# An S4 layer gated by a feed-forward block, forward and backward on one core: some transposing loads turned on TensorE, two dx chunks added in place, another order of the work

## The chip, the cores and the metric

The kernel runs on one core of a Trainium2 chip. The metric is the device time of one execution in microseconds. The time before is the median of three runs.

## The reference

The input `x` is 2048 rows of 512. It is layer-normed to `xn`; `xn` goes through an S4 convolution (a kernel of length 2048 for each of 512 channels, built from 128 complex states) and through a feed-forward block 512 to 1792 to 512. The output is `x + s * silu(ffn)`. The kernel returns this output and its gradients by `x`, by the six parameter arrays of the states (512 by 128 each), by the step and skip vectors and by both weights, for a given `grad_out`.

```python
def _A_ref(u, A_re, A_im, B_re, B_im, C_re, C_im, log_dt, Dskip):
    dt = jnp.exp(log_dt)[:, None]
    logdA, dB = dt * (A_re + 1j * A_im), dt * (B_re + 1j * B_im)
    P = jnp.exp(logdA[:, :, None] * arange(L))
    K = jnp.einsum("dn,dnl,dn->dl", C_re + 1j * C_im, P, dB).real
    y = irfft(rfft(pad(u)) * rfft(pad(K)))[:L]
    return y + u * Dskip

def _fwd(x, ...):
    xn = layernorm(x)
    s = _A_ref(xn, ...)
    g = silu(silu(xn @ w1) @ w2)
    return x + s * g

out, vjp = jax.vjp(_fwd, x, ...)
return (out, *vjp(grad_out))
```

## The kernel before

**Layout.** Rows are held as 128 partitions by 16 row tiles `t`, the 512 columns as four blocks of 128 (`b`, or `dk` and the like), the 1792 hidden columns as 14 tiles `ft`. The convolution is done by matrices of a discrete Fourier transform (`dft_fwd`, `cplx_mul`, `dft_inv`). Intermediates that don't fit on the chip go to DRAM and come back: `Hd` (hidden before silu, stored with hidden columns on the partitions), `DHd` (its gradient, in the same layout), `Pd` (the feed-forward part of the gradient by `xn`), `Yd` and `Ed` (powers of the state factors), `dKd` (gradient of the convolution kernel).

**Streams and order.** The work is written as generators, each named by one letter. A generator yields after each step, a step being a group of instructions, often for one engine. Seven strings, `PLAN[0]` to `PLAN[6]`, list the letters in the order in which the steps are issued; `play` walks through a string and advances the named generator by one step. Each engine carries out its instructions in the order in which they are issued, and SP, which issues most of the DMAs, does too. `SLOTS` fixes which of its buffers each tile takes, and `WAYS` says for each eviction made by `k.ev` whether ACT (`A`, line 112 in the profile) or DVE (`D`, line 113) makes it.

**Stages.** `PLAN[0]` is set-up and the start of the feed-forward block, `PLAN[1]` and `PLAN[2]` the forward convolution and the rest of the feed-forward block, `PLAN[3]` the backward convolution (`B`), the output (`O`) and the backward feed-forward block (`A`, `x`). The change touches mostly what follows.

- `gen_dx` (`x`, line 1166): sixteen row tiles of `dhT` times `W1`. Each result is evicted to `pd_s` and stored in `Pd`. `gen_conv_bwd` (`B`) writes the other part of the gradient by `xn`, called du, into `k.ds` on the chip.
- `gen_ssm_loads` (`Y`, line 970): sixteen groups `(b, h, q0)`. For each a tile `YT` is loaded from `Yd` by two transposing DMAs, and for each second group `Eb` from `Ed`. `gen_ssm_fold` (`N`) makes `Gf` from `dKd`.
- `gen_ssm_v` (`V`, line 996): `YT` times `Gb` into the PSUM tile `ps_v` (pool `pc`, two buffers), evicted to `Vb`.
- `gen_ssm_products` (`T`, lines 1012 and 1017): complex products of `Vb` with `Eb` on DVE, four multiplications into `Tp` and `Tq` and two sums, six instructions a group.
- `gen_ssm_sums` (`S`, line 1034): `Tp` summed over its `NE` = 21 exponents by matmuls with the identity, two exponents at a time (eleven matmuls), into `psS`, copied to `Sa`. `gen_ssm_grads` (`Z`) adds the two halves of `Sa` (line 1059) and makes the six state gradients and that of the step.
- `gen_dw2_loads` (`h`), `gen_dw2_turns` (`t`) and `gen_dw2` (`w`, line 1206): for each `ft`, `h_in` is loaded from `Hd`, brought to rows on the partitions, put through silu into `a_tok`, and multiplied with `k.do`. The tiles `ft` 0 to 8 are loaded plain (line 1182) and turned by sixteen TensorE transposes (line 134), with silu from PSUM in two halves (line 1197); 9 to 13 are loaded by a transposing DMA (line 1180), with silu in one piece (line 1194).
- `gen_dw1_loads` (`g`, line 1221) and `gen_dw1` (`v`, line 1235): `dh_tok` comes from `DHd` by transposing DMAs, two for each of seven pairs, and is multiplied with `xn`.
- `gen_ln_loads` (`i`), `gen_ln_sums` (`k`, lines 1270 to 1277) and `gen_ln_rows` (`m`): the backward layer norm, in eight chunks of two row tiles. Chunks of `Pd` come back as `pd_l`; line 1270 adds `k.ds` on DVE and sums the row in the same instruction.

`PLAN[4]` mixes the end of `A` and `x` with the start of `N Y V T S`, `PLAN[5]` the rest of these with `Z h t w g v`, `PLAN[6]` the end of `t w g v` with `i k m`. The tiles of `i k m` take the memory of those of `N Y V T S Z`.

Of the kernel before, what the change touches and what calls it, by code (L numbers as in the profile page):

```python
# [18 lines left out]
P = 128  # L19
# [8 lines left out]
122p13273555417652067776357p577511777p747701636770773677J0J767p5787777367F66766767077F78676777633FF736746687F46F8F7486FF  # L28
F8F6666FF6F688FF56F64FJ8/XFXQFJFFFXXXPJXPXFXPFFFPXPXFPFPFQJFFFQQF9QQQFFFXFQFJQQXXQPFQXRPFFRXPXRRXFXPPFRFXPJFRRXFRPXFRQQQ
RPXQFQRQFXFRQQFFRFUFFXFQXFFFFRQRXRPRFRQXRRJPRRUPFPXRRURFRPRURQRXRFJRQCRPQFXXXXFFRQXXXQFQFQQXPQRPPFCRCCCFFFRCRCQRPCRQFRFC  # L30
RFFRFFPQRQCUQFRCFFFFCQQRFFCCQQCFCQFCXRCQQCFQCRPXFFCRXCFXCFXFPXCRPFXFCXRFCXRFJCFRRCXRPCXCFRFFQQCFRFCQQFCFRQPFFCRQPRRFCPQC
QFXFRQQRPQRCXRRRCXXJPRXRRXCUPXPRXXRCRFCPCCRQQPFFCFCFFCCPQCQFFQCRRQQCQRRXFQFCXFRFFCFQFCFCFCCCCPQJRRXCXRCCFCFFXPRRCXFPCRXC
CFCXQQCQFFQJRXPQFRCCQXCCCRQFRFQFCPRQCQRRRRRQRRRXRFPCFXRPFRFCXRCXPFURRRCXCFFRRXCCFFQFQJQQCXFXCFFCCRQCFFRCCRQQCQRFQCFRCRRR
RRCCCCXRQCCCCRCJRCRCRURRFCRRFCRCCRFFCCCCRC/CGCFCCGCCGFGFFFCCFCGCCGFGCCFGGCFCFFCGCGFCCGFCFWGCGGGGCGCFCHFCFGCGHFCCFCFCCGCH
FCGCWWCFCCCGGCWCWCCCWWHCCWCDHWHHGCCWDGMCCCWHCWWDWWDWDWLDGDWWDWWWWLWDMDDDMDDDLDDMLLWM/DEWDadDodDEDdDsBDADAAAoBDaDADdaAAAo
AsDBAoBABDWDWABADBBAasBoAAAoBBBAAAAlOBBADOaABoAADlOBBBsBxBoBDoBBDBBDEABABxDOABABxOABBBBAsxBODBoxDBxdOOBloDBoDOBxBaxDBBBD
# [17 lines left out]
101010101010101010101010101010101010101010101010101010101010101010110101010101011010101010101010101010101010101010101;tb
l.tv=01011101010110100010110100011010;tbl.ts=01010101110111010101001000101010;tbl.W=01010101010010100101;dft.t4=01001010
1010;gate.g=30124567;gate.S=01;da.doT=01010101;dftb.w8b=1010;da.dhT8=01201201;go.go_s=01010101;da.dhT6=10101010;go.go_r=
010101;go.go_g=01010101;da.pd_s=0101010101010101;go.go_x=01201201;sb.YT=0101010101010101;sb.Eb=10101010;sb.Gb=01010101;s
b.Vb=0101010101010101;sb.Tp=1010101010101010;sb.Sa=0101;fw.h_in=01010101010101;fw.a_tok=01010101010101;fw.o11=0120120120
1201;fw.dh_tok=0120120;fw.o10=0101010;lw.pd_l=01230123;lw.Gt=01230123;lw.m=01010101;lw.o1=12301230
# [4 lines left out]
WAYS = """J=DAADADAA;  # L64
F=DAAAAAAAADAAAAAAAAAAAAAAAAADAAAADAAAAAAADAAAAAAAAAAAAAADDAAAAAAADADDDAAA;
X=AAAAAAAAAAAAAAAAAAAAAAAAAAAAADDA;
U=AD;
R=DAAAAADDAAAADADAAADDAADDDADAAAAAAAAADAAAAAADAAAA;
C=DAADAAAAAAAAAAAAAAAADDAAAAAAAAAAAAAADDADAAADDADAADADDDADAAAAAAAA;
W=ADDDDDADDDDDDD;  # L70
D=ADAADDAAAADAAAAAAAAAAAAADAADAAAAAAAAAADA;
d=DADDDAAD;
B=ADAAAAAAAAAAAAADAAAAAAAAAAAAAAAAAAAADADAAAAAAAAAAAAADAAA;
x=AAAAADAAAADAAAAA;
V=ADDAAADDAAAAAAADAAAAAAAAAAAAAAAAAAAAAAAAAAAAAAAAAAAAAAAAAAAAAAAA;
w=ADAAAAAAAAAAAA;
v=AAAAAAAAAADAAADAAAAAAAAAAAAA"""
# [82 lines left out]
def setup_tiles(k, wp):  # L160
# [51 lines left out]
def gen_plain_consts(k, w):  # L212
# [7 lines left out]
    G.memset(k.pi[:], PI_LO)  # L220
# [680 lines left out]
def gen_conv_bwd(k):  # L901
# [3 lines left out]
    for b in range(4):  # L905
# [55 lines left out]
def gen_ssm_loads(k, sb, groups):  # L961

    nc = k.nc
    for i, (b, h, q0) in enumerate(groups):
        if i == 2:
            k.par = load_params(k, sb)
            yield
        YT = sb.tile([P, 2, 8, P], BF16, name="YT", tag="YT", bufs=2)
        for c in range(2):
            nc.sync.dma_start_transpose(YT[:, c], k.Yd[b, h][:, (c * 16 + q0) * P:(c * 16 + q0 + 8) * P])  # L970
# [34 lines left out]
def gen_ssm_products(k, sb, groups):  # L1005

    for i, (b, h, q0) in enumerate(groups):
        Vb, E = k.Vb.pop(i), k.Eb[b, h]
        Tp = sb.tile([P, NE, 2, 16, 4], BF16, name="Tp", tag="Tp", bufs=2)
        Tq = sb.tile([P, NE, 2, 16, 4], BF16, name="Tq", tag="Tq")  # L1010
        for o, r, c, ec in ((Tp, 0, 0, 0), (Tq, 0, 1, 1), (Tp, 1, 0, 1), (Tq, 1, 1, 0)):
            k.nc.vector.tensor_tensor(out=o[:, :, r].rearrange("p e (q w) a -> p q w e a", w=2),  # L1012
                                      in0=Vb[:, :, c].rearrange("p q w (e a) -> p q w e a", a=4),
                                      in1=E[:, ec, q0:q0 + 8].unsqueeze(2).to_broadcast([P, 8, 2, NE, 4]), op=ALU.mult)
            yield
        for r, op in ((0, ALU.subtract), (1, ALU.add)):
            k.nc.vector.tensor_tensor(out=Tp[:, :, r], in0=Tp[:, :, r], in1=Tq[:, :, r], op=op)  # L1017
# [5 lines left out]
def gen_ssm_sums(k, sb, groups):  # L1023

    nc = k.nc
    for i, (b, h, q0) in enumerate(groups):
        Tp = k.Tp.pop(i)
        if i % 4 == 0:
            Sa = sb.tile([P, 2, 2, 2, 4, 32], F32, name="Sa", tag="Sa", bufs=2)
        psS = k.pt.tile([P, 2, 2, 64], F32, name="psS", tag="pt")  # L1030

        for e in range(0, NE, 2):
            n = min(2, NE - e)
            nc.tensor.matmul(out=psS[:, 0:n].rearrange("p z r x -> p z (r x)"), lhsT=k.ident[:],  # L1034
                             rhs=Tp[:, e:e + n].rearrange("p z r x a -> p z (r x a)"), start=(e == 0), stop=(e + 2 >= NE))
        yield
        nc.scalar.copy(out=Sa[:].rearrange("p z r w a q -> p (z r) (w a) q")[:, :, :, 16 * h + q0:16 * h + q0 + 8],
                       in_=psS[:].rearrange("p z r (q x) -> p (z r) x q", q=8))
# [5 lines left out]
def gen_ssm_grads(k, b, sb):  # L1044
# [14 lines left out]
    TT(out=fl(S[:, 0]), in0=fl(S[:, 0]), in1=fl(S[:, 1]), op=ALU.add)  # L1059
    TT(out=u2[:], in0=C, in1=two(B, 1), op=ALU.mult)  # L1060
    yield
    S0, S1 = (fl(S[:, 0])[:, :, w] for w in (0, 1))
# [39 lines left out]
    ddt = sb.tile([1, P], BF16, name="ddt", tag="ddt")  # L1102
    TT(out=ddt[:], in0=pd[:], in1=k.dt[0:1, bs], op=ALU.mult)
    yield
    k.st(k.outs[8].unsqueeze(0)[:, bs], ddt[:])
# [51 lines left out]
def gen_dx(k, da):  # L1157
    nc = k.nc
    D, FT = k.D, k.FT
    for c in range(k.T // 2):  # L1160
        dhs = k.dhT[c, 0], k.dhT[c, 8]
        for t in range(2):
            pd = da.tile([P, D], BF16, name="pd_s", tag="pd_s", bufs=2)
# [4 lines left out]
            yield  # L1168
            k.ev(pd[:], ps[:])
# [5 lines left out]
def gen_dw2_loads(k, fw):  # L1175

    for ft in range(k.FT):
        h = fw.tile([P, k.T, P], BF16, name="h_in", tag="h_in", bufs=2)
        if ft >= 9:
            k.nc.sync.dma_start_transpose(h[:], k.Hd[ft])  # L1180
        else:
            k.nc.sync.dma_start(h[:].rearrange("p t n -> p (t n)"), k.Hd[ft])
# [4 lines left out]
def gen_dw2_turns(k, fw):  # L1187

    for ft in range(k.FT):
# [3 lines left out]
        if ft >= 9:  # L1193
            k.nc.scalar.activation(out=a[:], in_=h[:], func=ACT.Silu)  # L1194
            yield
            continue
# [248 lines left out]
```

## Time and profile before

| | |
|---|---|
| median of three runs | 581.04 us |
| the three runs | 576.36, 581.04, 586.96 us |
| profiled execution, its own time | 581.0 us |
| span of the profiled execution | 578.5 us |
| mean granted TensorE clock | 0.981 |
| busy: PE, DVE, ACT, POOL | 520.2, 518.0, 451.3, 78.3 us |
| bytes moved by DMA | 145.75 MB, 252 GB/s |

The span runs from the first to the last instruction; the profiled execution's own time is a little longer. PE is TensorE's matmuls and PEld its weight loads; SPq is SP's queue as it issues DMAs. A row of a group gives the line, engine, operation, tiles, shapes and count, then the busy time in us and the mean of one in ns, then the idle time of the engine just before and what ended it.

### The profile page before, as it was taken

How to read it: one execution, taken by the hardware profiler on the slowest of the kernel's cores; microseconds unless marked ns; L12 is line 12 of the kernel's file. 1: busy time of each engine (PE TensorE's matmuls, PEld its weight loads, DVE VectorE, ACT ScalarE, POOL GpSimd, SP SyncE). 2: the span in 40 equal slices, each digit the busy share in tenths (PEclk: the TensorE clock that was granted, in tenths of full speed). 3: DMA queues.
4: the chain of work that ended last, by engine and by line, in shares of the span. 5: the costliest groups of instructions: out<-in, count | busy, mean ns of one | idle time of the engine just before them, and what ended most of it. 6: DMA issues, size and time to landing. Idle time of an engine off the chain costs nothing. (4 is left out here: it accounts for less than half of the span.)

```text
span 578.5 us, 13917 instructions
## 1 busy us (share of the span) xinstructions
PE 520.2 (90%) x5681; PEld 385.6 (67%) x5704; DVE 518.0 (90%) x814; ACT 451.3 (78%) x560; POOL 78.3 (14%) x168
## 2 busy tenths in 40 slices
PE   1497999998998989999999999999799979999983
PEld 1365768676777766876677766777567858776752
DVE  8989999999999768999999889778899989983984
ACT  7999999999998749999899866754578766643553
POOL 4321101011102030000000000000002202123221
PEclk9889999999999999999999999999899999999998
DMA  8977798988898996788779899979999999999991
GB/s 242 330 300 229 233 231 310 302 226 252 329 263 250 342 295 268 239 270 247 255 261 300 245 307 287 238 180 244 234 231 234 214 208 213 230 222 245 215 284 74
DMA packets 174032, 145.75 MB, mean 252 GB/s; under 512 B 102224, under 2 KB 151632, under 8 KB 170896
## 3 DMA queue, kind: packets, MB, share of 16 engines
q1 hardware_dynamic: 164656, 122.05, 79.0%
q0 software_dynamic: 6768, 19.93, 9.6%
q10 hardware_dynamic: 2544, 2.88, 1.5%
q8 instruction: 44, 0.72, 0.5%
q14 instruction: 20, 0.16, 0.1%
HBM read 58.72 MB, written 59.90 MB: 205 GB/s over the span
## 5 line engine op out<-in xcount | busy, mean ns | idle before, releaser
L112 ACT CAST dA<-ps_s 128x1024 bf16<-128x1024 f32 x84 | 84.4, 1034 | 7.5 <-PE ps_s L399 4.8
L755 PE MATMUL ps_h<-XT,W 128*128 128x256 bf16 x448 | 61.4, 288 | 11.4 <-ACT hT L112 8.2
L112 ACT CAST Vb<-ps_v 128x672 bf16<-128x672 f32 x59 | 41.5, 730 | 27.5 <-PE ps_v L996 17.0
L755 PEld LDWEIGHTS <-W 128*128 128x128 bf16 x448 | 44.5, 103 | 20.8 <-issue 12.9
L1146 PE MATMUL ps_da<-doT,W 128*128 128x256 bf16 x448 | 56.8, 273 | 0.0
L1235 PE MATMUL ps_w<-dh_tok,xn 128*128 128x256 bf16 x448 | 52.4, 273 | 3.7 <-ACT o L112 1.9
L1206 PE MATMUL ps_w<-YD,a_tok 128*128 128x512 bf16 x211 | 48.9, 379 | 3.7 <-ACT a_tok L1194 2.7
L1166 PE MATMUL ps_dx<-W,dhT 128*128 128x512 bf16 x224 | 51.0, 379 | 0.0
L1235 PEld LDWEIGHTS <-xn 128*128 128x128 bf16 x448 | 43.1, 98 | 10.7 <-issue 2.9
L772 PE MATMUL ps_o<-W,aT 128*128 128x512 bf16 x214 | 49.0, 379 | 1.4 <-ACT aT L763 0.5
L112 ACT CAST dB<-ps_i 128x1024 bf16<-128x1024 f32 x41 | 41.2, 1030 | 9.7 <-PE ps_i L444 8.9
L1146 PEld LDWEIGHTS <-W 128*128 128x128 bf16 x448 | 41.3, 98 | 8.5 <-issue 2.1
L1149 DVE TENSOR_TENSOR dhT<-ps_da,dhT 128x512 bf16<-128x512 f32 x56 | 37.5, 684 | 6.8 <-PE ps_da L1146 6.4
L1206 PEld LDWEIGHTS <-a_tok 128*128 128x128 bf16 x224 | 21.3, 98 | 27.0 <-ACT a_tok L1194 3.3
L772 PEld LDWEIGHTS <-aT 128*128 128x128 bf16 x224 | 21.2, 98 | 26.6 <-issue 1.6
L1166 PEld LDWEIGHTS <-dhT 128*128 128x128 bf16 x224 | 21.3, 98 | 23.4 <-issue 0.4
L996 PE MATMUL ps_v<-Gb,YT 128*128 128x168 bf16 x256 | 28.0, 242 | 3.9 <-DMA YT<-Yd 2.0
L1012 DVE TENSOR_TENSOR Tp<-Vb,Eb 128x1344 bf16<-128x1344 bf16 x32 | 27.3, 854 | 4.5 <-ACT Vb L112 3.7
L399 PEld LDWEIGHTS <-TF 128*128 128x128 bf16 x384 | 25.0, 101 | 8.5 <-issue 5.2
L574 ACT ACTIVATE sn<-V 128x2048 bf16<-128x2048 int16 (+1 forms) x16 | 30.2, 1885 | 0.3
L470 DVE TENSOR_TENSOR cm<-sp_in,dA 128x2048 bf16<-128x2048 bf16 x24 | 29.3, 1221 | 0.9
L472 DVE TENSOR_TENSOR sp_in<-sp_in,dA 128x2048 bf16<-128x2048 bf16 x24 | 29.3, 1221 | 0.6
(232 smaller groups left out, 1214.7 us busy)
## 6 DMA issues: line engine op xcount, KB each, us to landing
Yd<-YD SPq DMA_DIRECT2D x8, 1024.0 KB, 5.1
sp_in<-Ud SPq DMA_DIRECT2D x8, 1024.0 KB, 6.2
Ed<-ds SPq DMA_DIRECT2D x8, 672.0 KB, 4.0
Eb<-Ed SPq DMA_DIRECT2D x8, 672.0 KB, 6.2
h_in<-Hd SPq DMA_DIRECT2D x9, 512.0 KB, 5.2
Hd<-hT POOLq DMA_DIRECT2D x8, 512.0 KB, 4.8
Ud<-dA SPq DMA_DIRECT2D x8, 512.0 KB, 7.3
KXd<-dA SPq DMA_DIRECT2D x4, 1024.0 KB, 5.4
```

The costliest lines, as they stand in the source:

```text
L112: return self.nc.scalar.copy(out=out, in_=in_)
L470: TT(out=t2[:], in0=b[:, :, gs], in1=a[:, 1:2, gs].to_broadcast([P, 2, n, P]), op=ALU.mult)
L472: TT(out=b[:, :, gs], in0=b[:, :, gs], in1=a[:, 0:1, gs].to_broadcast([P, 2, n, P]), op=ALU.mult)
L574: nc.scalar.activation(out=sn[:, 0:n], in_=low, func=ACT.Sin, scale=-2 * PI_LO / 2.0 ** PB)
L755: nc.tensor.matmul(out=ps[:, j], lhsT=k.W1[:, dk, ft * P:ft * P + P], rhs=XTv[:, :, dk, :], start=(dk == 0), stop=(dk == DK - 1))
L772: nc.tensor.matmul(out=ps[:], lhsT=aT[:, ft, t * P:t * P + P], rhs=k.W2[:, ft, :], start=(ft == 0), stop=(ft == FT - 1))
L996: nc.tensor.matmul(out=ps[:, u, 168 * c:168 * c + 168], lhsT=YT[:, c, q + u, :], rhs=Gb[:, q0 + q + u].rearrange("p w x -> p (w x)"), star ...
L1146: nc.tensor.matmul(out=ps[:, j], lhsT=k.W2[:, ft, dk * P:dk * P + P], rhs=dTv[:, :, dk, :], start=(dk == 0), stop=(dk == DK - 1))
L1149: nc.vector.tensor_tensor(out=dh[:, i0:i0 + 2, :], in0=ps[:], in1=dh[:, i0:i0 + 2, :], op=ALU.mult)
L1166: nc.tensor.matmul(out=ps[:], lhsT=dhs[ft // 8][:, ft % 8, t * P:t * P + P], rhs=k.W1[:, :, ft * P:ft * P + P], start=(ft == 0), stop=(ft ...
L1206: nc.tensor.matmul(out=ps[:], lhsT=at[:, t, :], rhs=k.do[:, t, :], start=(t == 0), stop=(t == k.T - 1))
L1235: nc.tensor.matmul(out=ps[:], lhsT=k.xn[:, t, dk * P:dk * P + P], rhs=dh[:, t].rearrange("p j n -> p (j n)"), start=(t == 0), stop=(t == k ...
```

## The change

- `h_in` is always loaded plain and turned by TensorE. In every fourth group of `Y` (3, 7, 11, 15) each of the two halves of `YT` is loaded plain into `Yn` (one buffer), turned by eight transposes into a PSUM tile of the pool `pc` and evicted by `k.ev`.
- The last four row tiles of `gen_dx` (chunks 6 and 7) are not evicted and stored: one DVE instruction adds the PSUM tile to `k.ds` in place and sums the row into `k.mx`. The layer-norm steps of these chunks load no `pd_l` and leave out line 1270.
- The matmuls of `gen_ssm_sums` take one exponent at a time, 21 of them, into a `psS` of half the size; `Sa` is half as large, and line 1059 is gone. The products use one `Tq` for both parts, of half the size, and their order changes accordingly.
- `ddt` is written into memory of `acc`; an unused constant goes.
- The seven strings of `PLAN`, the `SLOTS` and the `WAYS` are new. Up to `PLAN[3]` the streams are the same as before but for `x`; the number of steps of each stream in the first three strings differs by at most two.

```diff
 PLAN = """
-122p13273555417652067776357p577511777p747701636770773677J0J767p578...
+13212255p35274656675167770J376p67756J4777163777737FF077p07136F1377...
...
-WAYS = """J=DAADADAA;
+WAYS = """J=DADDADDD;
...
-x=AAAAADAAAADAAAAA;
-V=ADDAAADDAAAAAAADAAAAAAAAAAAAAAAAAAAAAAAAAAAAAAAAAAAAAAAAAAAAAAAA;
-w=ADAAAAAAAAAAAA;
-v=AAAAAAAAAADAADAAAAAAAAAAAAAA"""
+x=AAAAADAAAAAD;
+V=DAAADADAAAAAAAAAAAAAAAAAAAAAAAADAADAAAAAAAAAAAAAAAAAAAAAAAAAAAAA;
+Y=DAADDADA;
+w=DDAADDADADAADA;
+v=ADAAAAAAAAAADAAAAAAAAADAAAAA"""
...
@@ gen_ssm_loads
         YT = sb.tile([P, 2, 8, P], BF16, name="YT", tag="YT", bufs=2)
+        if i % 4 == 3:
+            for c in range(2):
+                Yn = sb.tile([P, 8, P], BF16, name="Yn", tag="Yn")
+                nc.sync.dma_start(Yn[:].rearrange("p q x -> p (q x)"), k.Yd[b, h][:, (c * 16 + q0) * P:(c * 16 + q0 + 8) * P])
+                yield
+                pt = k.pc.tile([P, 8, P], BF16, name="pt_y", tag="pc")
+                for j in range(8):
+                    nc.tensor.transpose(out=pt[:, j], in_=Yn[:, j], identity=k.ident[:])
+                yield
+                k.ev(YT[:, c], pt[:])
+                if c == 0:
+                    yield
+            k.YT[i] = YT
+            yield
+            continue
         for c in range(2):
             nc.sync.dma_start_transpose(YT[:, c], ...)
@@ gen_ssm_products
-        Tq = sb.tile([P, NE, 2, 16, 4], BF16, name="Tq", tag="Tq")
+        Tq = sb.tile([P, NE, 16, 4], BF16, name="Tq", tag="Tq")
...
@@ gen_ssm_sums
-        for e in range(0, NE, 2):
-            n = min(2, NE - e)
-            nc.tensor.matmul(out=psS[:, 0:n]..., lhsT=k.ident[:], rhs=Tp[:, e:e + n]..., start=(e == 0), stop=(e + 2 >= NE))
+        for e in range(NE):
+            nc.tensor.matmul(out=psS[:]..., lhsT=k.ident[:], rhs=Tp[:, e]..., start=(e == 0), stop=(e == NE - 1))
@@ gen_ssm_grads
-    TT(out=fl(S[:, 0]), in0=fl(S[:, 0]), in1=fl(S[:, 1]), op=ALU.add)
...
-    ddt = sb.tile([1, P], BF16, name="ddt", tag="ddt")
+    ddt = acc[:].bitcast(BF16)[0:1, 0, 0:P]
@@ gen_dx
+            late = c >= 6
...
+            if late:
+                r, i = 2 * c + t, 2 * (c - 6) + t
+                nc.vector.scalar_tensor_tensor(out=k.ds[:, r, :], in0=ps[:], scalar=1.0, in1=k.ds[:, r, :],
+                                               op0=ALU.mult, op1=ALU.add, accum_out=k.mx[:, i, 0:1])
+                yield
+                continue
             k.ev(pd[:], ps[:])
             yield
             nc.sync.dma_start(k.Pd[:, 2 * c + t, :], pd[:])
@@ gen_dw2_loads
-        if ft >= 9:
-            k.nc.sync.dma_start_transpose(h[:], k.Hd[ft])
-        else:
-            k.nc.sync.dma_start(h[:].rearrange("p t n -> p (t n)"), k.Hd[ft])
+        k.nc.sync.dma_start(h[:].rearrange("p t n -> p (t n)"), k.Hd[ft])
@@ gen_dw2_turns
-        if ft >= 9:
-            k.nc.scalar.activation(out=a[:], in_=h[:], func=ACT.Silu)
-            yield
-            continue
@@ gen_ln_loads
+        pd = k.ds[:, 2 * c:2 * c + 2, :]
+        if c < 6:
+            pd = lw.tile([P, 2, k.D], BF16, name="pd_l", tag="pd_l", bufs=4)
+            nc.sync.dma_start(pd[:], k.Pd[:, 2 * c:2 * c + 2, :])
@@ gen_ln_sums
+            if c < 6:
                 STT(out=pd[:, i], in0=pd[:, i], scalar=1.0, in1=k.ds[:, t, :], ..., accum_out=m[:, i, 0:1])
```

More of the change, by code (lines that the diff above doesn't have):

```diff
@@ L32 @@
[L32 to L36, printed above, removed]
@@ L54 @@
[L54 to L58, printed above, removed]
@@ new lines @@
+010101010101010101010010101010101101010101010010101010101010101010101001010101010101010101010101010101010101000010101010
+101010101011010;tbl.tv=01011101110101100010010101100101;tbl.ts=01010101010111010101001000101010;tbl.W=010101010100101001
+01;dft.t4=010011001010;gate.g=30124567;gate.S=01;da.doT=01010101;dftb.w8b=1010;da.dhT8=01201201;go.go_s=01010101;da.dhT6
+=10101010;go.go_r=010101;go.go_g=01010101;da.pd_s=101010101010;go.go_x=01201201;sb.YT=0101010101010101;sb.Eb=01010101;sb
+.Gb=01010101;sb.Vb=1010101010101010;sb.Tp=0101010101010101;sb.Sa=0101;fw.h_in=01010101010101;fw.a_tok=01010101010101;fw.
@@ L1028, in gen_ssm_sums @@
         if i % 4 == 0:
-            Sa = sb.tile([P, 2, 2, 2, 4, 32], F32, name="Sa", tag="Sa", bufs=2)
-        psS = k.pt.tile([P, 2, 2, 64], F32, name="psS", tag="pt")
-        for e in range(0, NE, 2):
-            n = min(2, NE - e)
-            nc.tensor.matmul(out=psS[:, 0:n].rearrange("p z r x -> p z (r x)"), lhsT=k.ident[:],
-                             rhs=Tp[:, e:e + n].rearrange("p z r x a -> p z (r x a)"), start=(e == 0), stop=(e + 2 >= NE))
+            Sa = sb.tile([P, 2, 2, 4, 32], F32, name="Sa", tag="Sa", bufs=2)
+        psS = k.pt.tile([P, 2, 64], F32, name="psS", tag="pt")
+        for e in range(NE):
+            nc.tensor.matmul(out=psS[:].rearrange("p r x -> p (r x)"), lhsT=k.ident[:],
+                             rhs=Tp[:, e].rearrange("p r x a -> p (r x a)"), start=(e == 0), stop=(e == NE - 1))
         yield
-        nc.scalar.copy(out=Sa[:].rearrange("p z r w a q -> p (z r) (w a) q")[:, :, :, 16 * h + q0:16 * h + q0 + 8],
-                       in_=psS[:].rearrange("p z r (q x) -> p (z r) x q", q=8))
+        nc.scalar.copy(out=Sa[:].rearrange("p r w a q -> p r (w a) q")[:, :, :, 16 * h + q0:16 * h + q0 + 8],
+                       in_=psS[:].rearrange("p r (q x) -> p r x q", q=8))
         if i % 4 == 3:
@@ L1058, in gen_ssm_grads @@
     TT(out=u1[:], in0=C, in1=two(B, 0), op=ALU.mult)
[L1059 removed]
     TT(out=u2[:], in0=C, in1=two(B, 1), op=ALU.mult)
     yield
[L1062 removed]
+    S0, S1 = (fl(S[:])[:, :, w] for w in (0, 1))
     BC = k.par[:, 2:6, bs]
@@ L1101, in gen_ssm_grads @@
     yield
-    ddt = sb.tile([1, P], BF16, name="ddt", tag="ddt")
-    TT(out=ddt[:], in0=pd[:], in1=k.dt[0:1, bs], op=ALU.mult)
+    ddt = acc[:].bitcast(BF16)[0:1, 0, 0:P]
+    TT(out=ddt, in0=pd[:], in1=k.dt[0:1, bs], op=ALU.mult)
     yield
-    k.st(k.outs[8].unsqueeze(0)[:, bs], ddt[:])
+    k.st(k.outs[8].unsqueeze(0)[:, bs], ddt)
     yield
@@ L1162, in gen_dx @@
         for t in range(2):
-            pd = da.tile([P, D], BF16, name="pd_s", tag="pd_s", bufs=2)
+            late = c >= 6
+            if late and k.du_end != (3, 8):
+                raise ValueError("du is not there yet")
+            if not late:
+                pd = da.tile([P, D], BF16, name="pd_s", tag="pd_s", bufs=2)
             ps = k.pf.tile([P, D], F32, name="ps_dx", tag="pf")
@@ L1291, in gen_ln_rows @@
         yield
-        TT(out=o1[:], in0=o1[:], in1=pd[:], op=ALU.add)
+        TT(out=o1[:], in0=o1[:], in1=pd[:, 0:2], op=ALU.add)
         yield
```

87 lines of the change are left out of this document (47 added, 40 removed).

## The prediction

> **What bounds the kernel now.** I read the page first, then the busy time by stretches, then the rows of single lines, and the chain of waits last.
>
> ```profile
> span 578.5 us, 13917 instructions
> ...
> PE 520.2 (90%) x5681; PEld 385.6 (67%) x5704; DVE 518.0 (90%) x814; ACT 451.3 (78%) x560; POOL 78.3 (14%) x168
> ```
>
> TensorE and VectorE are both busy for 90% of the span, so no engine alone is the bound. The table by stretches (stretch, its length, then busy time of PE, PEld, DVE, ACT and POOL, granted clock, DMA share, GB/s) tells where they are not:
>
> ```profile
> 0.00:10.90 10.90, 0.02 (x1) 0.03 (x2) 9.46 (x34) 7.85 (x12) 5.34 (x54) 1.00 0.81 204
> 10.90:360.00 349.10, 324.32 (x3928) 240.15 (x3940) 327.20 (x456) 313.16 (x358) 41.10 (x58) 0.98 0.87 274
> 360.00:400.00 40.00, 39.45 (x434) 29.87 (x429) 31.37 (x41) 24.30 (x27) 0.52 (x1) 1.00 0.95 224
> 400.00:570.00 170.00, 156.22 (x1330) 115.50 (x1340) 149.37 (x286) 105.60 (x164) 30.27 (x54) 0.99 1.02 224
> 460.00:480.00 20.00, 16.62 (x151) 11.72 (x151) 17.64 (x31) 12.06 (x18) 1.87 (x3) 1.00 1.10 239
> 480.00:500.00 20.00, 19.95 (x202) 16.62 (x202) 18.67 (x32) 14.88 (x28) 5.56 (x10) 1.00 1.07 215
> 535.00:555.00 20.00, 19.13 (x142) 14.03 (x144) 19.66 (x50) 11.54 (x21) 4.36 (x8) 1.00 1.12 215
> ```
>
> The reader should take three numbers from it. From 400 to 570 us, the part that this change rewrites, PE is idle for 170.00 - 156.22 = 13.8 us. Between its first work and 360 us it is idle for 349.10 - 324.32 = 24.8 us. And in 400 to 570 the DMA share is 1.02, above all other long stretches: the queues, too, are full there. In a stretch where nothing was late (480 to 500) PE was idle for 0.05 us; in the one before it for 3.38.
>
> What was late there is seen in the chain (start, length, what):
>
> ```profile
> 427.71 0.29 PE ps_v L996 x4
> ...
> 429.87 3.40 PE ps_w L1206 x15
> 433.27 0.45 PE pt_t L134 x8
> ...
> 439.89 1.15 PE psS L1034 x11
> ...
> 458.77 6.39 SPq L1221
> ...
> 466.56 7.24 DMA YT<-Yd
> ```
>
> The two long pieces, 6.39 and 7.24 us, are SP's queue issuing a transposing DMA and one landing; the short ones are the PE work that I use below. The rows of the lines say why. In each, min/median/max is in ns and then the count follows; the landing rows belong, in order, to L1180 and L1182:
>
> ```profile
> L970 SPq DMA_TRANSPOSE YT<-Yd x32: 1237/1381/3552, 362.7 to 494.1; - x32
> L1180 SPq DMA_TRANSPOSE h_in<-Hd x5: 2702/2907/6190, 510.5 to 553.7; - x5
> L1182 SPq DMA_DIRECT2D h_in<-Hd x9: 370/578/936, 410.3 to 497.0; - x9
> L1221 SPq DMA_TRANSPOSE dh_tok<-DHd x14: 2010/2930/6394, 415.0 to 539.9; - x14
> L1171 SPq DMA_DIRECT2D Pd<-pd_s x16: 319/336/2567, 274.2 to 409.9; - x16
> ...
> DMA to landing us min/median/max: 5.9/7.8/10.4
> ...
> DMA to landing us min/median/max: 4.6/5.2/6.4
> ```
>
> The same 512 KB of h_in cost SP's queue 2.9 us as a transpose and 0.58 us plain, and land after 7.8 against 5.2 us. SP issues in order, so every load behind a transpose is late by that much. All transposes of the second half by their medians are 32 x 1.38 + 14 x 2.93 + 5 x 2.91 = 99 us of SP in about 190 us.
>
> **The change, part by part.**
>
> *Loads turned by TensorE.* The five transposed h_in (ft 9 to 13) become plain loads, and of the sixteen YT groups numbers 3, 7, 11 and 15 are loaded plain, in two halves each. SP loses 5 x 2.91 + 8 x 1.38 = 25.6 us and gains 13 x 0.58 = 7.5 us (for the eight YT halves, which have no plain row, I take the h_in row, of twice their size). PE gains 5 x 16 + 8 x 8 = 144 transposes; eight took 0.45 us (433.27 in the chain), so 18 x 0.45 = 8.1 us. PE is 92% busy there, so I put all of it on the path. The Trainium skill (TensorE: Matmul & The Clock Gate, Part 4: PE-mode transpose) gives about 275 ns for one in a kernel, so that 144 would be some 40 us and the sum below 32 us longer; the row of eight in 0.45 us disagrees, and the trace decides.
>
> The other engines, and ps_dx (224 matmuls in sixteen rows of 51.0 / 16 = 3.2 us):
>
> ```profile
> L1166 PE MATMUL ps_dx<-W,dhT 128*128 128x512 bf16 x224 | 51.0, 379 | 0.0
> L1197 ACT ACTIVATE a_tok<-pt_t 128x1024 bf16<-128x1024 bf16 x18 | 18.6, 1041 | 0.6 <-PE pt_t L134 0.5
> L1270 DVE SCALAR_TENSOR_TENSOR pd_l<-pd_l,ds 128x512 bf16<-128x512 bf16 x16 | 11.0, 686 | 6.5 <-DMA out_dram<-gout 4.9 <-DMA pd_l<-Pd 1.6
> L1194 ACT ACTIVATE a_tok<-h_in 128x2048 bf16<-128x2048 bf16 x5 | 9.6, 1913 | 7.0 <-DMA h_in<-Hd 7.0
> L112 ACT CAST pd_s<-ps_dx 128x512 bf16<-128x512 f32 x14 | 8.3, 591 | 11.6 <-issue 9.6 <-PE ps_dx L1166 1.8 <-ACT dhT L1124 0.2
> L113 DVE COPY W<-pt_t 128x1024 bf16<-128x1024 bf16 x12 | 7.8, 683 | 0.0
> L1059 DVE TENSOR_TENSOR Sa<-Sa 128x512 f32<-128x512 f32 x4 | 2.7, 684 | 0.8 <-ACT Sa L1037 0.8
> L1270 DVE DVE_READ_ACCUMULATOR pd_l<-pd_l,ds 128x1 f32 x16 | 1.3, 82 | 0.0
> ```
>
> Silu of h_in goes from 5 x 1.91 to 10 x 1.04 on ACT, +0.8 us; the eight YT evictions are four on DVE (4 x 0.683 = 2.7) and four on ACT (4 x 1.04 = 4.2). ACT is idle for 64 us of the 170, which hides its share. The gain is the waits: PE's 13.8 us of idle time. Since 480 to 500 shows that the interleaving runs with next to none when data are there, I let 3.0 us remain: -10.8 us. Its bounds are 0, if the waits stay, and -13.8.
>
> *Last two dx chunks.* Four evictions (591 ns, all on ACT) and four Pd stores (0.34 us of SP) go; four DVE instructions reading PSUM come in stage 4. No row has this operation from PSUM; the nearest is L1270 with 686 + 82 ns, so 4 x 0.768 = 3.1 us on DVE, where 360 to 400 has 8.6 us of idle time to hide it; uncovered it costs those 3.1. The same four L1270 leave the end, with two of eight loads. From 535 to 555 DVE is busy for 19.66 of 20 us, tighter than PE, so these 3.1 us are on the path: -3.1, from 0 to -3.1.
>
> *State sums.* Eleven matmuls, ten of 256 columns and one of 128, become 21 of 128. Eleven took 1.15 us; 21 at the pace of the transposes take 1.18. Sixteen times the difference is +0.5 us of PE. The copy of the sums halves, on ACT, where idle time hides it either way; L1059 goes (2.7 us of DVE). In all PE is given 8.6 us more. Reordering the six products to share one half-sized Tq adds no instruction; DVE runs them in order already. That ddt is written into acc adds no wait, since it waits for the matmul that reads acc anyway; the memset that goes is POOL's, busy for 14%.
>
> DVE is the check on this. Over the state-gradient stage:
>
> ```profile
> 386.90:512.00 125.10, 116.16 (x1039) 87.11 (x1045) 115.37 (x182) 80.72 (x125) 16.89 (x31) 0.99 1.05 227
> ```
>
> Idle 9.7 us. New on DVE are at most 2.7 (YT), 3.1 (dx) and, from the new ways of w, five instead of one of its evictions there (four more, at 0.69 as L1270 for the same size, 2.8), less three L1059 (2.1): +6.5, which fits, with 3.2 us to spare.
>
> *Order anew.* The strings for the first 360 us hold nearly the same steps as before; their places differ. PE's idle 24.8 us there is what an order can change. I take a quarter back, -6.2 us: an estimate, and the least certain term. Bounds: -12 (half of it) and +8 (a third more waiting).
>
> **Sum.** The profiled execution took 581.0 us, 2.5 above its span, and equals the median of the three runs, 581.04 (576.36 to 586.96). 581.0 + 8.6 - 10.8 - 3.1 - 6.2 = **569.5 us**. Its own bounds, taken together by half: 562 to 577.
>
> **Rivals.**
>
> *The order gives more.* The same with -12 instead of -6.2 and the last 3.0 us of waits gone as well: 569.5 - 5.8 - 3.0 = 560.7 us. For it speaks that DVE, ACT and PE are all below 94% from 10.9 to 360; against it that 360 to 400 shows PE full already (39.45 of 40), and that DVE allows the middle stage only 3.2 us.
>
> *The waits stay.* What remains of transposes on SP, 24 of YT and 14 of dh_tok by their medians, is still 74 us, and dh_tok, not YT, was the piece of 6.39 us in the chain. Then PE pays 8.6 us for nothing and only the end gains: 581.0 + 8.6 - 3.1 = 586.5 us. The Trainium skill (Advanced Engine Details and Errata, X-Bar Transpose (TRN2)) says that transposing DMAs are as fast as regular ones here; by that rule this rival would hold. The landing rows, 7.8 against 5.2 us, speak against it.
>
> *The halves of YT hold up TensorE (slower).* Yn has one buffer. The second half can't be issued before the first half's eight transposes have run, and those transposes stand in PE's own order, so whatever follows them on PE waits: ps_v, then Vb, then the products on DVE. In the new order PE has between the two turns, by the rows shown, for group 3 one ps_dx (3.2), two ps_v (0.29 each) and a psS (1.15), 4.9 us; for group 7 one ps_w (3.4), two ps_v and two turns of h_in (0.45 each), also 4.9; for 11 and 15 about 7, since a psS, a ps_w and another ps_w or psS stand there.
>
> The median landing is 5.2 us plus the issue, so groups 3 and 7 have no margin and 11 and 15 under 2 us. If SP stands on a dh_tok transpose at that moment (up to 6.39 us), each group loses about 6.3 us, or its two halves about 3.2 each: 4 x 6.3 = 25 us, 569.5 + 25 = 594.5 us. It decides from the point at which SP is late by more than 2 us at most of the four. For it: SP's longest issues of YT and dh_tok, 3.55 and 6.39 us. Against it: less stands on SP than before, and the order can issue ahead for the first halves.
>
> **How the numbers follow.** What a measurement of this kernel can tell from no change is about 2%, so from 569.4 to 592.7 us counts as the same. The forecast has 0.48 and lies on that border, so half of it is faster (0.24) and half the same (0.24). More from the order: 0.16, all faster. Waits stay: 0.11, the same. Halves hold up TensorE: 0.25, slower. So faster 0.40, same 0.35, slower 0.25. The range runs from 557 to 596: it leaves out about 0.05 below (the order's rival with an end of 3 us more) and about 0.12 above. The forecast's own range is 562 to 577.
>
> **What would show it.** Right: PE's idle time from 400 us to its last matmul falls below 5 us; the chain has no DMA YT piece above 3 us; SP issues 24 and 14 transposes and no h_in one; a_tok waits for no h_in; DVE is still above 92% in the middle stage; the last layer-norm steps have four L1270 fewer. PE's idle time from its first work up to 360 us is near 19 us. Wrong: PE waits for Yn, at the transposes of YT, for more than 2 us a group (the slower rival); PE's idle time from 400 on stays at 12 us or more (the waits stay); or 10.9 to 360 gets longer, so that the term for the order has the wrong sign.

## The result and the profile after

The changed kernel takes 581.8 us (median of 12 runs, 580.18 to 582.91), the kernel before 577.0 (median of its 12 runs beside them; 578.4 to 578.9 in the batches of 23 to 31 runs beside the experiments). Ratio 1.0076, 95% interval 1.0055 to 1.0098: 0.8% slower, where 569.5 us, 2% faster, was forecast. The ratio leaves out the slowest run of the kernel before, 586.96 us, which counts as slow and is one of the three behind the forecast's 581.04. The profiled execution took 580.7 us.

From here "before" in a table is the execution that the prediction showed, which was 2 to 4 us slower than the medians of its kernel. Line numbers are those of the changed kernel, some 15 to 25 above the old ones in the second half and four lower there in e6 (L135 the transposes on TensorE, L113 and L114 evictions on ScalarE and VectorE, L1012 `ps_v`, L1293 the old L1270).

Page of the changed kernel, the first lines:

```profile
span 578.9 us, 14495 instructions
...
PE 527.7 (91%) x5982; PEld 394.9 (68%) x6008; DVE 528.9 (91%) x822; ACT 444.4 (77%) x556; POOL 76.8 (13%) x167
```

PE has 7.5 us more to do (520.2 before) and the span is 0.4 us longer, so idle time did go away somewhere. Table by stretches, changed kernel, columns as in the prediction:

```profile
10.90:360.00 349.10, 321.91 (x3894) 237.29 (x3905) 328.53 (x456) 309.46 (x358) 39.05 (x57) 0.98 0.89 270
400.00:570.00 170.00, 164.45 (x1650) 126.47 (x1662) 160.47 (x298) 105.05 (x163) 30.36 (x54) 1.00 0.95 230
200.00:215.00 15.00, 14.84 (x235) 13.02 (x233) 11.34 (x13) 9.40 (x13) 6.22 (x11) 1.00 1.02 295
215.00:240.00 25.00, 18.81 (x204) 11.39 (x204) 18.16 (x22) 17.97 (x21) 0.86 (x1) 0.86 0.80 283
```

From 400 to 570 PE is idle for 5.55 us instead of 13.8. From 10.9 to 360 it is idle for 27.2 us instead of 24.8. One stretch stands out, 215 to 240: three engines lose 4.7 to 6.1 us each against the kernel before, and the granted clock is 0.86. It follows a stretch in which the new order does better, 200 to 215. The same two before:

```profile
200.00:215.00 15.00, 12.25 (x171) 9.45 (x170) 9.57 (x12) 7.23 (x12) 6.19 (x11) 1.00 0.97 293
215.00:240.00 25.00, 24.18 (x293) 17.85 (x292) 22.81 (x29) 24.02 (x26) 0.86 (x1) 0.93 0.71 256
```

What each engine waited for in 215 to 240 in the changed kernel (us in all, times, longest), and SP's own queue in 200 to 225:

```profile
ACT g L797 <- DMA YD<-Od: 5.0, 1, 5.0
PE ps_s L427 <- ACT dA L113: 4.7, 1, 4.7
```

```profile
SPq L716 <- DVE S_b L114: 4.7, 1, 4.7
```

SP's queue in order of time (start, length, what):

```profile
208.00 1.49 SPq L789 DMA_DIRECT2D YD<-Od  x3
214.24 0.32 SPq L716 DMA_DIRECT2D Sd<-S_b  x1
214.66 3.33 SPq L789 DMA_DIRECT2D YD<-Od  x4
```

Read from below: the store of `S_b` stands at SP's head for 4.7 us until VectorE has evicted `S_b`. Behind it wait four of the seven loads of `Od`. ScalarE reaches the gate's fourth Silu (L797) before the fourth load has landed and stands for 5.0 us; the next instruction in ScalarE's order is an eviction of `dA`, and TensorE needs that. So a store whose data TensorE never reads has stopped it through two queues. In the kernel before, five of the seven loads stand ahead of the store, and the Silus begin at 218 us instead of 215; no Silu waits there, although the store stands at SP's head for 4.9 us there too.

By the places of three steps (the first transform of `ds`, the first `ps_v`, the last `psS`, and the end of the span), the trace of before has 235.3, 382.1, 513.5 and 578.5 us, that of after 239.9, 386.3, 521.7 and 578.9. So the first part is 4.6 us longer, the middle 0.4 shorter, the state stage 4.0 longer and the tail 7.8 shorter. From the first `ps_v` to TensorE's last matmul, before (two lines: up to the last `psS` and in all) and after:

```profile
382.10:513.50 131.40, 122.46 (x1103) 92.90 (x1110) 119.54 (x188) 82.72 (x128) 17.04 (x31) 0.99 1.03 223
...
382.10:570.20 188.10, 174.31 (x1478) 129.15 (x1489) 164.73 (x306) 113.49 (x174) 30.32 (x55) 0.99 1.01 224
```

```profile
386.30:521.70 135.40, 130.57 (x1372) 101.29 (x1382) 127.16 (x202) 84.96 (x128) 18.07 (x33) 1.00 0.99 231
...
386.30:571.90 185.60, 180.03 (x1772) 137.76 (x1786) 171.30 (x313) 111.29 (x171) 31.44 (x56) 1.00 0.93 224
```

In this pair of traces the stretch has become 2.5 us shorter: TensorE works 5.7 us more and idles 8.2 us less (13.8 and 5.6). Behind the last matmul the span has 7.0 us left, before 8.3.

### The profile page after: what moved, and what is told of

The parts are those of the page before. It is cut to its first block, busy times and chain, and to the rows that moved or that the text cites. A ratio compares the mean times of both kernels' runs of the same rounds, so it can differ in the third digit from the quotient of the medians.

```text
span 578.9 us, 14495 instructions
## 1 busy us (share of the span) xinstructions
PE 527.7 (91%) x5982; PEld 394.9 (68%) x6008; DVE 528.9 (91%) x822; ACT 444.4 (77%) x556; POOL 76.8 (13%) x167
## 5 line engine op out<-in xcount | busy, mean ns | idle before, releaser
L113 ACT CAST dA<-ps_s 128x1024 bf16<-128x1024 f32 x82 | 82.1, 1029 | 5.6 <-PE ps_s L427 3.4
L113 ACT CAST Vb<-ps_v 128x672 bf16<-128x672 f32 x59 | 41.5, 727 | 38.6 <-PE ps_v L1012 26.8
L772 PE MATMUL ps_o<-W,aT 128*128 128x512 bf16 x212 | 50.3, 385 | 3.0 <-ACT aT L763 1.6
L113 ACT CAST dB<-ps_i 128x1024 bf16<-128x1024 f32 x38 | 38.3, 1032 | 7.9 <-PE ps_i L444 7.8
L1012 PE MATMUL ps_v<-Gb,YT 128*128 128x168 bf16 x256 | 27.1, 236 | 4.6 <-ACT Vb L113 1.7
L1214 ACT ACTIVATE a_tok<-pt_t 128x1024 bf16<-128x1024 bf16 x28 | 28.8, 1038 | 2.4 <-PE pt_t L135 2.2
L399 PEld LDWEIGHTS <-TF 128*128 128x128 bf16 x384 | 23.8, 98 | 7.0 <-ACT TF L281 2.4
```

The lines of the kernel that those rows point to most:

```text
L113: return self.nc.scalar.copy(out=out, in_=in_)
L772: nc.tensor.matmul(out=ps[:], lhsT=aT[:, ft, t * P:t * P + P], rhs=k.W2[:, ft, :], start=(ft == 0), stop=(ft == FT - 1))
L1214: yield from turned(k, lambda t: h[:, t], k.T, a, lambda out, in_: k.nc.scalar.activation(out=out, in_=in_, func=ACT.Silu))
```

## The experiments

**Which half of the order loses.** Two hybrids: the changed kernel with the order of before for the first three of its seven stages (up to about 240 us), and the kernel before with the changed order there.

```diff
 # e1_early_old: the changed kernel; e2_late_old: the same the other way round
-PLAN[0:3], their slots and ways as changed
+PLAN[0:3], their slots and ways as before
```

> The changed kernel with the first three strings of the order, their buffers and their eviction ways as before (up to about 250 us), everything later as changed. Theory O: 4 us faster than the changed kernel, 577 to 578 us, level with before. Theory P: no change, 581 to 582 us.

> The kernel before with the first three strings, their buffers and ways as in the changed kernel, everything later as before. Theory O: 4 us slower than before, 581 us. Theory P: as before, 577 us.

Measured: e1 577.2 us, ratio 0.9992 (0.9961 to 1.0023); e2 583.0 us, ratio 1.0079 (1.0044 to 1.0113). Stretch 215 to 240 of e1, then of e2, and first `ps_v` to last matmul in e1:

```profile
215.00:240.00 25.00, 24.25 (x291) 17.58 (x290) 22.32 (x28) 24.10 (x26) 1.30 (x2) 0.94 0.75 279
```

```profile
215.00:240.00 25.00, 19.35 (x215) 11.69 (x213) 18.41 (x23) 18.22 (x21) 0.86 (x1) 0.86 0.75 275
```

```profile
383.70:569.10 185.40, 180.84 (x1786) 137.74 (x1786) 171.24 (x313) 111.25 (x171) 31.33 (x56) 1.00 0.95 224
```

The same chain stands in e2's trace: ScalarE waits 4.8 us for the load, TensorE 4.5 us for `dA`. The loss goes with the order of the first three stages, whole. The rest of the change (transposes, sums, dx in place, order from stage 4 on) makes its stretch as short as in the changed kernel, 185.4 us, but gains nothing that the times can tell. A repeat of the kernel before, in one profile, was to tell whether the trace shown was typical:

> The kernel before, unchanged, for another profile: the profiled execution shown took 581.0 us, and the median of twelve runs is 577.0. Theory O (the order of the first 360 us costs, the rest is even): a typical execution of before reaches the first ps_ds matmul near 235 us and the last matmul near 566. Theory P (the added TensorE work costs, the first 360 us are even): a typical execution reaches the first ps_ds matmul near 239 us, like the changed kernel, and ends 4 us earlier than shown because of its second half.

It took 578.6 us. Its first transform of `ds` was at 234.3, as theory O says, and its last matmul ended at 568.7, 1.5 us earlier than in the trace shown and later than the 566 of theory O.

**Do the transposes on TensorE cost their time?** Each of the 144 new ones runs twice.

```diff
-                for j in range(8):
+                for j in [*range(8), *range(8)]:
                     nc.tensor.transpose(out=pt[:, j], in_=Yn[:, j], identity=k.ident[:])
```

(and likewise in the turning of `h_in`, ft 9 to 13)

> The changed kernel with each of its 144 new transposes carried out twice (8.1 us more TensorE work at 0.056 us each, the same data, nothing else changed). Theory O needs the added transposes to be paid on the path but returned by the waits: 6 to 8 us slower than the changed kernel, 588 to 590 us. If TensorE's added work is hidden, at most 2 us slower, 582 to 584 us.

Measured 588.5 us, ratio 1.0156 (1.0114 to 1.0198). First `ps_v` to last matmul:

```profile
386.90:579.40 192.50, 188.31 (x1930) 145.80 (x1930) 171.61 (x313) 111.18 (x171) 31.33 (x56) 1.00 0.93 216
```

TensorE has 8.3 us more to do than in the changed kernel (188.31 - 180.03), and the stretch is 6.9 us longer. (The changed kernel's trace has records of 1772 matmuls here and e1's, with the same work, of 1786; against e1's 180.84 us it is 7.5 us.) The estimate of 8.1 us for 144 transposes holds nearly, and TensorE's own time is on the path here nearly in full. So the change pays for its transposes and must win as much from waits.

**The chain of three queues.** If the store of `S_b` is what stopped TensorE, it is enough to let the loads pass it.

```diff
 # e4_loads_first, stage 3 (G: gate rows; its first seven are the loads of Od)
-CCGFGCCGCFFFFFCCCCCFGWFGGCGGFF
+CCGFGCCGGGGGCFFFFFCCCCCFWFCGFF
```

> The changed kernel with one edit: in the third stage the four last loads of Od into YD (L789) are issued right behind the first three, so ahead of the store of S_b (L716) on SP's queue. In the trace of the changed kernel that store waits 4.7 us for VectorE at SP's head, the four loads go out behind it at 214.7, ScalarE's fourth Silu of the gate (L797) then waits 4.97 us for them at 224.7, and TensorE stands 4.7 us behind ScalarE's next eviction. Theory Q (this one chain of three queues is what the early order lost): TensorE busy in 215 to 240 back from 18.8 to 23 or more, first transform of ds at 235 to 236 instead of 239.9, time 577 to 578. Rival S (the loss is spread: the rows before, at 177 and at 196, were already 4 to 6 us late, and the stall only fills time that would be lost anyway): first transform of ds stays at 238.5 or later, time 580 to 582.

Measured 573.6 us (572.55 to 575.28), ratio 0.9947 (0.9912 to 0.9982). The same kernel again, with more runs:

> The kernel of e4 once more in five rounds, for a narrower interval and to stand beside e10 on one chip: 572 to 575, ratio to the kernel before 0.988 to 0.998.

574.6 us, ratio 0.9944 (0.9920 to 0.9969). SP's queue and the stretch 215 to 240 in this second profile:

```profile
207.70 4.79 SPq L789 DMA_DIRECT2D YD<-Od  x7
214.01 0.32 SPq L716 DMA_DIRECT2D Sd<-S_b  x1
```

```profile
215.00:240.00 25.00, 23.30 (x310) 16.98 (x310) 23.89 (x31) 23.84 (x28) 0.86 (x1) 1.00 0.83 311
```

The seven loads go out in one piece, the stretch is full again, and the first transform of `ds` is at 233.8 us (232.0 in the first profile) instead of 239.9. Theory Q had 577 to 578 us; the two times are some 3 us below that. Rival S has fallen. The time is below both kernels.

The second way to break the chain leaves SP as it is and takes the link on ScalarE away:

```diff
 # e8_silu_later, stage 3: the fourth and fifth Silu behind an eviction of dA and the activation aT
-HGGCCGCCCCMHGFCCGFGCFGCLCCCFCGFC
+HGGCCCCCCMHFCCGFGCFGCLCCGGCFCGFC
```

> The changed kernel with one edit: the loads of Od into YD stay behind the store of S_b on SP's queue, but the fourth and fifth Silu of the gate (L797) come some ten steps later in the order, behind ScalarE's evictions of dA and aT. Theory Q (ScalarE's queue is the link through which the late loads reach TensorE): the 4.7 us in which TensorE stood behind ScalarE at 222 to 227 is gone or under 1.5 us, first transform of ds at 234 to 236.5, time 575 to 578. Rival S (the loads themselves are on the path: their rows are needed for ds soon after in any order): the wait moves to a later instruction, first transform of ds at 238 or later, time 580 or more.

Measured 577.0 us, ratio 0.9994 (0.9966 to 1.0022). The stretch 215 to 240, its waits, and SP's:

```profile
215.00:240.00 25.00, 21.67 (x285) 15.42 (x284) 22.23 (x29) 22.17 (x25) 0.86 (x1) 1.00 0.81 292
```

```profile
ACT g L797 <- DMA YD<-Od: 1.6, 2, 1.3
```

```profile
SPq L716 <- DVE S_b L114: 4.2, 1, 4.2
```

SP still stands for 4.2 us, but ScalarE only for 1.6, TensorE's 4.7 us wait is gone, and the first transform of `ds` is at 234.95. So both links are shown: SP's store holds the loads, and ScalarE's place in its own order decides whether TensorE sees it.

**What bounds the second half.** VectorE was 94% busy there. One edit gives it less to do:

```diff
 # e5_evict_act
-Y=DAADDADA;
-w=DDAADDADADAADA;
+Y=AAAAAAAA;
+w=ADAAAAAAAAAAAA;
```

> The changed kernel with one edit: the evictions of dw2 on ScalarE as before (one of 14 on VectorE instead of seven) and all eight evictions of the turned Y on ScalarE (four were on VectorE). VectorE has some 6 x 0.64 + 4 x 0.69 = 6.6 us less to do between 385 and 560. Theory D (VectorE, 94% busy there, sets the pace of the state stage): last psS sum at 515 to 517 instead of 521.7, time 575 to 577. Rival E (TensorE's own work sets the end from 400 on, VectorE only shares the pace): time 580 to 583. Rival F (ScalarE's queue then holds up the V evictions): 584 or more.

Measured 582.3 us, ratio 1.0082 (1.0043 to 1.0122), level with the changed kernel. First `ps_v` to last matmul:

```profile
386.90:573.70 186.80, 180.01 (x1772) 137.84 (x1786) 165.41 (x303) 117.98 (x181) 31.34 (x56) 1.00 0.93 222
```

VectorE is freed of 5.9 us (171.30 to 165.41), and the stretch is 1.2 us longer, not shorter. TensorE's work is the same, 180.01 us. Theory D's 575 to 577 us did not come. What VectorE gave up went to ScalarE (111.29 to 117.98 us), so the run shows that moving this work wins nothing; that VectorE alone sets no pace here is likely, not shown.

**The two loads, each by the transposing DMA again.**

```diff
 # e6_y_by_dma: groups 3, 7, 11, 15 of Y        # e7_h_by_dma: h_in of ft 9 to 13
-nc.sync.dma_start(Yn..., k.Yd[b, h]...)
-nc.tensor.transpose(...)  x8, and the eviction
+nc.sync.dma_start_transpose(YT[:, c], k.Yd[b, h]...)
```

> The changed kernel with one edit: the four groups of Y that it loads plain and turns on TensorE are loaded with the transposing DMA again, issued at the place of the plain loads; 64 transposes and eight evictions of 1024 columns are gone. Theory P1 (TensorE sets the end from 400 on, so each transpose taken away is time won, 64 x 0.056 = 3.6 us): time 577 to 579. Rival W1 (the transposing loads land late and TensorE or VectorE waits for YT, as before the change): PE idle in 400 to 570 up from 5.5 to 9 or more, time 582 to 586.

> The changed kernel with one edit: the five last row tiles of h (ft 9 to 13) come by the transposing DMA again and one Silu of 2048 columns each; 80 transposes on TensorE are gone. Theory P1 (TensorE sets the end): 80 x 0.056 = 4.5 us won, time 576.5 to 578.5. Rival W1 (SP is held by five issues of some 6 us and the loads land late; TensorE waits for a_tok): PE idle in 400 to 570 up from 5.5 to 10 or more, time 581 to 586.

Measured: e6 581.2 us, ratio 1.0063 (1.0023 to 1.0102); e7 580.4 us, ratio 1.0054 (1.0018 to 1.0091). Both intervals take in the changed kernel's 1.0076, so neither the gain nor the loss that the expectations name is shown. First `ps_v` to last matmul in e6, with two of its PE waits between 400 and 572, then in e7:

```profile
385.50:571.70 186.20, 176.44 (x1708) 134.22 (x1722) 169.22 (x309) 107.26 (x168) 31.36 (x56) 1.00 0.96 222
```

```profile
PE ps_w L1248 <- DMA dh_tok<-DHd: 2.1, 1, 2.1
...
PE ps_v L1008 <- DMA YT<-Yd: 1.7, 1, 1.7
```

```profile
387.90:572.10 184.20, 176.08 (x1692) 133.12 (x1706) 171.14 (x313) 110.81 (x167) 30.86 (x56) 1.00 0.96 225
```

In e6 PE has 3.6 us less to do, just the 64 transposes, and idles 4.2 us more (9.8 against 5.6); the two rows shown make 3.8 us, where the changed kernel has 0.3 of waits for transposing loads. In e7 it has 4.0 us less to do and idles 2.5 more. The exchange is nearly even: a transpose on TensorE and the wait that it spares cost about the same here, as far as these intervals tell. To see whether that holds without the early stall, both edits went on top of e4's:

> The kernel of e4 (the four loads of Od ahead of the store of S_b) and on top of it the edits of e6 and e7, so that Y and h are loaded as before the change and the 144 transposes are gone again; what is left of the change is the order, the sums by single exponents and dx in place. If the turning by TensorE is worth nothing either way (e6 and e7 moved the time by some 1 us each, inside their intervals): 571 to 574, level with e4 to 0.3%. If the transposes are a cost that only the stall had covered: 566 to 570. If the transposing loads wait again once the stall is gone: 576 or more.

573.1 us, ratio 0.9933 (0.9903 to 0.9963), level with e11 (0.9944) inside the intervals. The even exchange holds without the stall too: the turning by TensorE won nothing that the times can tell. Both kernels are 0.6 to 0.7% below the kernel before, by the order, dx in place and the sums together, which no run takes apart further.

**dx in place.** The four last row tiles of dx are stored and loaded again.

```diff
 # e9_dx_stored
-nc.vector.scalar_tensor_tensor(out=k.ds[:, r, :], in0=ps[:], ..., accum_out=k.mx[:, i, 0:1])
+k.ev(pd[:], ps[:])
+nc.sync.dma_start(k.Pd[:, 2 * c + t, :], pd[:])
```

> The changed kernel with one edit: the four last row tiles of dx are evicted, stored and loaded again as the other twelve are, and the last two chunks of the layer norm add them to du as the others do (16 of L1293 in the tail instead of 12; the four adds in place at L1189 become evictions). Forecast's step (the four additions leave a tail that VectorE sets): time 3 us above the changed kernel, 584 to 587. Theory P2 (TensorE sets the tail, its last matmul ends after the last row of the layer norm either way): last matmul at 571 to 573, time 580 to 583.

Measured 590.6 us, ratio 1.0228 (1.0188 to 1.0268): 9 us above the changed kernel, more than either theory. Its SP queue, and what TensorE (from 400 to 430) and SP (from 380 to 430) waited for:

```profile
409.19 0.32 SPq L1189 DMA_DIRECT2D Pd<-pd_s  x1
409.60 3.15 SPq L935 DMA_DIRECT2D GE<-dKd  x4
413.01 0.39 SPq L1189 DMA_DIRECT2D Pd<-pd_s  x1
413.49 0.38 SPq L973 DMA_DIRECT2D Yn<-Yd  x1
```

```profile
PE pt_y L977 <- DMA Yn<-Yd: 5.0, 1, 5.0
```

```profile
SPq L1189 <- ACT pd_s L113: 5.7, 2, 5.6
```

The stores that I put back stand at SP's head for 5.6 us, waiting for their eviction, and the second half of `Yn` goes out at 413.5 instead of 409.0; TensorE stands for 5.0 us. This is the early chain once more, made by my edit, so the run does not price the step cleanly. What can be read apart from it is the tail: from the last `psS` to the end of the span it takes 587.1 - 527.7 = 59.4 us, in the changed kernel 578.9 - 521.7 = 57.2. The step is worth about 2.2 us at the end.

## Why the prediction was wrong

**The step that failed: "Order anew".** Forecast -6.2 us, bounds -12 to +8. The order of the first stages cost 4.6 us (e2: 583.0 against 578.4; the changed kernel against e1: 581.8 against 577.2). The term was taken from the amount of idle time that an order can change, a quarter of 24.8 us, and not from the order. The two strings could have been followed: ahead of the store of `S_b` the new one has three loads of `Od`, the old one five, and the Silus that read them come earlier. Without that one place, the new early order seems to gain: e11 against e1, 574.6 to 577.2, some 2.6 us, though the two intervals of the ratio, 0.9920 to 0.9969 and 0.9961 to 1.0023, overlap a little. So the sign of the idea was probably right, its size under half, and the loads placed behind one store outweighed it.

**Why one wait of 4.7 us cost six.** Granted clock in short stretches of the changed kernel (the column behind the five engines):

```profile
221.00:224.00 3.00, 0.62 (x4) 0.25 (x4) 2.85 (x4) 0.00 (x0) 0.00 (x0) 0.93 1.03 403
224.00:226.70 2.70, 0.00 (x0) 0.00 (x0) 0.55 (x1) 1.99 (x3) 0.00 (x0) 0.50 1.04 402
226.70:230.30 3.60, 3.24 (x10) 1.11 (x11) 3.03 (x4) 3.60 (x4) 0.00 (x0) 0.50 0.90 323
230.30:233.00 2.70, 2.70 (x15) 1.02 (x14) 0.00 (x0) 0.74 (x2) 0.00 (x0) 0.98 0.40 118
```

TensorE stops at 222.0 us; 1.5 us later the clock falls to 0.50, and it stays there for the first 3.6 us after work resumes. The 3.24 us of busy time in that stretch would have been half as long at full clock, 1.6 us lost; 4.7 + 1.6 = 6.3 us, and e11 shows 239.9 - 233.8 = 6.1, the first profile of the same kernel 239.9 - 232.0 = 7.9. The Trainium skill (TensorE: Matmul & The Clock Gate, Part 1: The HAM clock gate) states that one idle window of about 3.4 us halves the clock and that as long a busy one restores it. The trace agrees on the way back, half clock until 3.6 us after the wait. On the way down less was enough: in the trace of before TensorE stood for 2.7 us, up to 213.8 us, and the granted clock was 0.50 from 215.4 to 218.2; in e8 the longest wait in the stretch, 1.7 us, left it at 1.00. The prediction had no term for this.

**Transposes and waits, +8.6 and -10.8.** Their sum, forecast -2.2 us, came out at -2.5 in the pair of traces (188.1 to 185.6), but this nearness is partly luck. The same stretch with the second half as before takes 187.2 us in b0 and 183.1 in e2, and as changed 185.4 in e1 and e4 and 186.4 in e11. From the first transform of `ds` to the end of the span it is 341.1 to 343.2 us with the old second half and 338.8 to 340.2 with the new, so the new one gains 1 to 4 us, and e10 gives none of it to the turning by TensorE. In the pair, each part was too large by a little under three. The idle time fell by 8.2 us, to 5.6 and not to 3.0. TensorE's busy time rose by 5.7, although the transposes alone cost what was said (e3). The clock column has 0.99 before and 1.00 after; 1% of 174 us of work is 1.7 us that fewer waits may have given back, which was not tested apart. SP was relieved as worked out:

```profile
L986 SPq DMA_TRANSPOSE YT<-Yd x24: 1232/1334/4986, 374.4 to 488.7; - x24
L973 SPq DMA_DIRECT2D Yn<-Yd x8: 333/428/658, 401.8 to 498.3; - x8
L1203 SPq DMA_DIRECT2D h_in<-Hd x14: 319/432/579, 412.0 to 547.0; - x14
```

**The four L1270, -3.1.** Predicted as VectorE's, in a tail that VectorE sets. They are gone as said, and the four that replace them cost what L1270 cost (686 + 83 ns, reading PSUM):

```profile
L1293 DVE SCALAR_TENSOR_TENSOR pd_l<-pd_l,ds x12: 669/685/693, 531.7 to 556.3; 128x512 bf16<-128x512 bf16 x12
...
L1189 DVE SCALAR_TENSOR_TENSOR ds<-ps_dx,ds x4: 681/686/692, 393.6 to 412.0; 128x512 bf16<-128x512 f32 x4
L1189 DVE DVE_READ_ACCUMULATOR ds<-ps_dx,ds x4: 83/83/83, 394.2 to 412.6; 128x1 f32 x4
```

Yet the span behind TensorE's last matmul became only 1.3 us shorter (8.3 to 7.0), and e9 puts the step at some 2.2. What failed is the premise that VectorE alone sets the tail. In the kernel before, VectorE's last row was done only 0.4 us behind TensorE's last matmul, at 570.6 against 570.2 us (start, length, what):

```profile
568.30 1.91 PE L1235 MATMUL ps_w<-dh_tok,xn 128*128 128x256 bf16 x16
...
569.94 0.69 DVE L1292 TENSOR_TENSOR o<-o,pd_l 128x1024 bf16<-128x1024 bf16 x1
```

The end of the changed kernel:

```profile
564.73 7.15 PE L1252 MATMUL ps_w<-dh_tok,xn 128*128 128x256 bf16 x64
...
569.26 0.69 DVE L1315 TENSOR_TENSOR o<-o,ds 128x1024 bf16<-128x1024 bf16 x1
```

The last row of the layer norm is done at 569.95 us, TensorE's last matmul at 571.9. Once VectorE was relieved, TensorE, now 1.9 us behind it, set the end.

**The check on VectorE.** It was given 6.5 us more for the state stage and got 7.6 (119.54 to 127.16). That stage did grow, by 4.0 us, but VectorE is not shown to be the cause: over the whole second half, moving 5.9 us from it to ScalarE won nothing (e5), while some 8 us more on TensorE cost 6.9 (e3). TensorE has 8.1 us more to do in it (122.46 to 130.57), the new transposes and matmuls of `ps_w` that stood in the tail before, and the tail is 7.8 us shorter.

**The sum.** It began at 581.0 us, the median of three runs; the medians of the later batches are 578.4 to 578.9. Against that the early order cost 4.6 instead of giving 6.2, a miss of 10.8 us. The late terms were to give 5.3 (-2.2 and -3.1); the profiles of before and after show 3.8 (2.5 and 1.3), and the times only 1.2 (578.4 to 577.2 in e1, 583.0 to 581.8 from e2 to the changed kernel), a miss of 4.1 with zero inside the interval. 10.8 + 4.1 less the 2.6 us of the baseline are the 12.3 us between 569.5 and 581.8.

**The rivals.** "The halves of YT hold up TensorE" did not come: TensorE waited for no load of `Yn` in the changed kernel. But e9 shows that its mechanism is real, with one wait of 5.0 us as soon as SP stands for 5.6 us at the wrong moment. "The waits stay" was wrong, since 8.2 us of waits went in the pair of traces (TensorE idles 5.6 us from 400 us to its last matmul, where the sign for right was under 5), though its 586.5 us is nearer to the result than the forecast. "The order gives more" was furthest off. Of the signs named in advance, the one against the forecast that came was that 10.9 to 360 would get longer.

## What to carry to other kernels

Where the order on the engines is written by hand, a store on a shared DMA queue is a wait for whoever fills its tile. Before such an order is changed, list for every store what stands behind it on that queue and which in-order engine reads those loads first. And a change that trades waits for work on the engine that sets the pace wins only the difference: count both with the same care, and start from the median of many runs.

## What the runs showed that I had not expected

The clock: an idle time of 4.7 us on TensorE cost 1.6 us more through 3.6 us at half clock. And an engine that is 92% busy over 186 us (VectorE) can hand 5.9 us to ScalarE without any gain while TensorE stands at 97% beside it.
